# One compact token list less: expert blocks read their token numbers from the regions

## The chip, the cores and the metric

The kernel runs on one core of one Trainium2 chip. The metric is device time in microseconds (us). The kernel before has a median of 954.01 us over 3 runs (950.93 to 955.18).

## The reference

Three stages in a row, for 4 sequences of 576 tokens (2304 tokens, width 512):

```python
# 1: causal attention (8 heads of 64) mixed with a linear memory
out = g * mem_out + (1 - g) * local
# 2: mixture of 8 experts, one expert per token
logits = x @ w_gate + modality_bias[modality_id]
e_idx = np.argmax(logits, axis=1)
for e in range(E):                       # E = 8
    mask = e_idx == e
    h = np.maximum(x[mask] @ w1[e], 0.0)  # 512 -> 1024
    out[mask] = gate_w[mask, None] * (h @ w2[e])
# 3: one dense network for all tokens, 512 -> 2048 -> 512
h = x @ w_in
g = np.where(h > 0.0, h, alpha * (np.exp(np.minimum(h, 0.0)) - 1.0))
return (g @ w_out)
```

Which tokens an expert gets is known only while the kernel runs, so the kernel has to build lists of token numbers and gather rows by them.

## The kernel before

The program is one long stream in three stages: attention (up to about 250 us of the trace), the experts (to about 535 us), the last network (to the end). Matrix products in 32 bits are made of three matmuls on a high and a low part of each operand, which is why there are many "split" steps: ScalarE (ACT) copies the high part, VectorE (DVE) or GpSimd (POOL) subtracts to get the low part.

**Lists.** While attention runs, the router gives each token an expert and a place. All the rows x (512 values and the gate weight) are stored in DRAM as `xd`. The number of each token is scattered into a list in DRAM, `idreg`: every expert has a region of 2560 places (`REG`) in it, and its tokens stand at the front of its region; the rest is zero. That is 18 scatters, one for each 128 tokens, each an indirect DMA from POOL that writes 128 numbers of 4 bytes (`scatter`, L84 to L92). After the first block of the first expert a second list is made in the same way, with 18 more scatters: `idc`, the compact list, in which the experts' tokens follow each other without holes, in the order in which the experts are worked on.

**Blocks.** An expert's tokens are worked on in blocks of 256 columns. For a block the queue of SyncE (SP) loads 256 token numbers into `gi`, POOL issues two indirect gathers of 128 rows each from `xd` into a buffer `xb` (or `xbh`, for the first block of the second expert), ACT and DVE scale the rows by the gate weight (`scale`, L901 and L902), TensorE (PE) turns them (`turn`, L911), and then the first layer (`hidden`, L928 to L931, tiles h and hs, eight steps f) and the second layer (L947, tile acc) run. The result goes to `y` at the block's place in the compact order.

**What else is hung into the blocks.** The functions of a block take lists of other work to be issued after a step. In the first expert's second block (`first(1)`) these are, among others: turning the raw 64-bit words of the last network's weights into 32-bit floats on DVE (`early_bits`, L1236 to L1240, tile T, three instructions for each quarter), and the loads of the second expert's weights (`wload`, L875). The quarter that matters below is loaded by `early_load(3)` (`load_half`, L1228, raw<-in_wout_dram, 512 KB) and used by `early_bits(3)`, which stands in DVE's order between the fifth hidden step's split and the sixth's (L931).

**Order.** All is in the order in which the program is written, per engine; a semaphore wait at the head of an engine's queue holds everything behind it. A DMA that SP issues waits on SP. DMAs from SP and from POOL run on the same 16 DMA engines.

**The last network.** 3 groups of 768 tokens times 16 chunks f of the hidden layer. During the first group each chunk loads the raw weights of the chunk two further on (`load`, fraw, two transfers of 512 KB) into one of two buffers, and DVE turns them (`conv`, L1236 to L1240). At the end of a group the rows are scattered to the output by token number (`finish`, L89, out_dram). The numbers for this, `idi`, are loaded once from `idc` (L1260), before the network's first load.

Of the kernel before, what the change touches and what calls it, by code (L numbers as in the profile page):

```python
# [10 lines left out]
F32 = mybir.dt.float32  # L11
F32R = mybir.dt.float32r
BF16 = mybir.dt.bfloat16
I32 = mybir.dt.int32
AF = mybir.ActivationFunctionType
ALU = mybir.AluOpType
# [68 lines left out]
def scatter(tc, key, dst, idx, src, spare):  # L85

    nc = tc.nc
    nc.gpsimd.memset(spare, 0.0)
    ins = nc.gpsimd.indirect_dma_start(dst, bass.IndirectOffsetOnAxis(ap=idx, axis=0), src, None)  # L89
    ins = ins.ins  # L90
    tc.declare_no_dep(ins, group=key, reason="the rows of the scatters are distinct")
    tc.add_to_no_dep_group(key, ins)  # L92
# [11 lines left out]
def attention_memory_moe_ffn_kernel(  # L104
# [21 lines left out]

    xd = dr.tile([NTOK, ROW], F32, name="xd")
    idreg = dr.tile([E * REG, 1], I32, name="idreg")
    idc = dr.tile([YW, 1], I32, name="idc")

    G = SimpleNamespace(**{k: v for k, v in locals().items() if k != "ctx"})
    ct = lambda name, shape, dt=F32: con.tile(shape, dt, name=name)
# [19 lines left out]
    G.keyE = ct("keyE", [128, E])  # L152
    G.tid = ct("tid", [128, NT], I32)
    G.rpi = ct("rpi", [128, NT], I32)
    G.cpi = ct("cpi", [128, NT], I32)
    G.run = ct("run", [128, E])
    G.spare = ct("spare", [1, 1])
    G.revE = ct("revE", [128, E])
# [4 lines left out]
    def late_constants():  # L163

        nc.gpsimd.memset(G.tri, 0.0)
        nc.gpsimd.affine_select(out=G.tri, in_=G.tri, pattern=[[1, 128]], compare_op=ALU.is_gt, fill=-1.0, base=0, channel_multiplier=-1)
        nc.vector.memset(G.ones, 1.0)
        nc.vector.memset(G.go, 1.0)

        for t0, K in GROUPS:  # L170
            nc.vector.memset(G.go[:, t0 * E : (t0 + K) * E].rearrange("p (e c) -> p e c", e=E)[:, :, 0], 0.0)
        for e in range(E):
            nc.gpsimd.memset(G.revE[:, e : e + 1], float(E - e))
            nc.gpsimd.memset(G.regE[:, e : e + 1], float(e * REG))
            nc.gpsimd.memset(G.iotE[:, e : e + 1], float(e))
            nc.gpsimd.memset(G.keyE[:, e : e + 1], float(e * REG * E + e))
            nc.gpsimd.memset(G.run[:, e : e + 1], float(e * REG))
        for t in range(NT):
            P2, r = divmod(t, 9)
            if r < 8:  # L180
                b, c = 2 * P2 + r // 4, r % 4
                nc.gpsimd.iota(G.tid[:, t : t + 1], pattern=[[0, 1]], base=b * S + 128 * c, channel_multiplier=1)
            else:
                for j in range(2):
                    nc.gpsimd.iota(G.tid[64 * j : 64 * j + 64, t : t + 1], pattern=[[0, 1]], base=(2 * P2 + j) * S + 512, channel_multiplier=1)
        zid = G.tmp[:, 0 : E * REG // 128].bitcast(I32)
        nc.vector.memset(zid, 0)
        nc.sync.dma_start(idreg.rearrange("(p f) o -> p (f o)", p=128), zid)
        nc.sync.dma_start(idc.rearrange("(p f) o -> p (f o)", p=128), zid[:, 0 : YW // 128])

    G.late_constants = late_constants

# [668 lines left out]
def define_experts(tc, G):  # L861
# [22 lines left out]
    def gather_rows(xb, gi, src, rows=NTOK, eng=nc.sync):  # L884
        eng.dma_start(gi, src)
        for h in range(2):
            nc.gpsimd.indirect_dma_start(xb[:, h, :], None, xd[0:rows, :], bass.IndirectOffsetOnAxis(ap=gi[:, h : h + 1], axis=0))  # L887
# [6 lines left out]


    def gather1(xb, gi, start):
        gather_rows(xb, gi, idc[bass.ds(start, BLK), :].rearrange("(p h) o -> p (h o)", h=2))


    def scale(xb):  # L900
# [98 lines left out]

def experts(tc, G, mp):  # L1000
    nc, ct = tc.nc, G.ct
    oh, rk, run, iotE, cpi = G.oh, G.rk, G.run, G.iotE, G.cpi
    wload, wsplit, gather0, gather1, scale, turn, block = G.wload, G.wsplit, G.gather0, G.gather1, G.scale, G.turn, G.block
    t8 = lambda n: ct(n, [128, E])
    key, rank, base, a88, b88 = t8("key"), t8("rank"), t8("base"), ct("a88", [128, E, E]), ct("b88", [128, E, E])
    inner = lambda v: v.unsqueeze(1).to_broadcast([128, E, E])
    outer = lambda v: v.unsqueeze(2).to_broadcast([128, E, E])
    info, infi = ct("info", [128, 3, E]), ct("infi", [128, 3, E], I32)
    nxt, nxti, end, iotJ = ct("nxt", [128, E, 8]), ct("nxti", [128, E, 8], I32), t8("end"), ct("iotJ", [128, 8])
    w, cpf = mp.tile([128, NT, E], F32, name="cw"), ct("cpf", [128, NT])  # L1010
    G.HT.append(mp.tile([128, 4, 2, BLK], F32R, name="hs4"))
    G.HS += [(G.HT[1][:, f, 0], G.HT[1][:, f, 1]) for f in range(4)]
    G.XH, G.XL = [mp.tile([128, 4, BLK], F32R, name=n) for n in ("xh", "xl")]
# [7 lines left out]
    def table_a():  # L1021
        nc.vector.tensor_tensor(run, run, G.regE, op=ALU.subtract)
        nc.vector.scalar_tensor_tensor(key, run, float(E), iotE, op0=ALU.mult, op1=ALU.subtract)
        nc.vector.scalar_tensor_tensor(key, G.first, 65536.0, key, op0=ALU.mult, op1=ALU.add)
        nc.vector.tensor_tensor(a88, inner(key), outer(key), op=ALU.is_gt)
        nc.vector.tensor_reduce(rank, a88, axis=AX.X, op=ALU.add)
        nc.vector.tensor_tensor(a88, a88, inner(run), op=ALU.mult)
        nc.vector.tensor_reduce(base, a88, axis=AX.X, op=ALU.add)
        nc.vector.tensor_tensor(b88, inner(rank), outer(iotE), op=ALU.is_equal)
        for r, src in enumerate((iotE, run, base)):  # L1030
            nc.vector.tensor_tensor(a88, b88, inner(src), op=ALU.mult)
            nc.vector.tensor_reduce(info[:, r], a88, axis=AX.X, op=ALU.add)
        nc.vector.tensor_copy(infi, info)


    def table_b():
        nc.vector.tensor_tensor(key, base, G.regE, op=ALU.subtract)
        for t0, K in GROUPS:
            nc.vector.tensor_tensor(w[:, t0 : t0 + K], oh[:, t0 * E : (t0 + K) * E].rearrange("p (e c) -> p c e", e=E), key.unsqueeze(1).to_broadcast([128, K, E]), op=ALU.mult)
        nc.vector.tensor_reduce(cpf, w, axis=AX.X, op=ALU.add)  # L1040
        nc.vector.tensor_tensor(cpf, cpf, rk, op=ALU.add)
        nc.vector.tensor_copy(cpi, cpf)

        for j in range(8):
            nc.gpsimd.memset(iotJ[:, j : j + 1], float(BLK * (j + 1)))
        nc.vector.tensor_tensor(end, info[:, 1], info[:, 2], op=ALU.add)
        nc.vector.tensor_tensor(nxt, iotJ.unsqueeze(1).to_broadcast([128, E, 8]), info[:, 2].unsqueeze(2).to_broadcast([128, E, 8]), op=ALU.add)
        nc.vector.tensor_scalar(nxt[:, 0], nxt[:, 0], float(FIRST + BLK), None, op0=ALU.add)
        nc.vector.tensor_tensor(nxt, nxt, end.unsqueeze(2).to_broadcast([128, E, 8]), op=ALU.min)
        nc.vector.tensor_copy(nxti, nxt)  # L1050

    why = dict(skip_runtime_bounds_check_because="a count of tokens")
# [5 lines left out]
        G.cnt[u] = nc.values_load(infi[0:1, 1, u : u + 1], min_val=0, max_val=NTOK, **why)  # L1058

    def start_of(u, j):  # L1060
        return nc.values_load(nxti[0:1, u, j : j + 1], engines=[mybir.EngineType.SP], min_val=0, max_val=NTOK, **why)

    P = lambda f, *a: (lambda: f(*a))
    mid1 = {}
# [21 lines left out]
    W[2][0] = G.kp.tile([128, 4096], F32R, tag="k1", name="W20")  # L1086
    load_eid(1)
    gather0(2)
    for t in range(NT):
        scatter(tc, "idc", G.idc, cpi[:, t : t + 1], G.tid[:, t : t + 1], G.spare)  # L1090
    wload(1, 0, 0)
    early_load(2)
    for g in mid2.get(4, ()):
# [1 line left out]
    early_bits(1)  # L1095
    wload(1, 0, 1)
    early_load(3)
    gather1(G.XBH, G.gis[2], nc.values_load(infi[0:1, 2, 1:2], engines=[mybir.EngineType.SP], min_val=0, max_val=NTOK, **why))

    def first(j):  # L1100
        mid1, mid2 = {}, {1: []}
# [141 lines left out]
def ffn(tc, G, ps, fp):  # L1243
# [13 lines left out]
    YL, EE = YL + ring("yk", 1, [4, 384], F32R), EE + ring("ef", 1, [384])  # L1257
    EG = ring("eg", 2, [384])
    GH, GL = ring("gh", 4, [384], F32R), ring("gl", 4, [384], F32R)
    nc.sync.dma_start(idi, idc[0:NTOK, :].rearrange("(t p) o -> p (t o)", p=128))  # L1260

    WS, YS, HP, GG, ACC = {}, {}, {}, {}, {}
    cnt = {}
# [55 lines left out]
    def gsplit(g, f, h):  # L1319
        gg = GG[g, f, h]  # L1320
        gh, gl = rot(GH, "gh"), rot(GL, "gl")
        nc.scalar.copy(gh, gg)
        eng = nc.vector if g and f < 2 or g == NG - 1 and f == NF - 1 else nc.gpsimd
        eng.tensor_tensor(gl, gg, gh.bitcast(F32), op=ALU.subtract)  # L1324
        GG[g, f, h] = (gh, gl)
# [28 lines left out]
    for i, (g, f) in enumerate(seq):  # L1354
        g1, f1 = seq[i + 1] if i + 1 < len(seq) else (NG, 0)
        f2 = f + 2 if g == 0 and f + 2 < NF else None
        if i > WM and g1 < NG:
            wsplit(g1, f1, 0)
        if f2 and f2 > 3:
            load(f2)  # L1360
        mm1(g, f, 0)
        if f2 and i > 1:
            conv(f2, 0)
        elu(g, f, 0)
        if i < 2:
            conv(2, 2 * i)
        if i > 0:
            gsplit(*seq[i - 1], 1)
        if 0 < i <= WM:
            wsplit(g1, f1, 0)  # L1370
        if f2 and i > 1:
            conv(f2, 1)
        mm1(g, f, 1)
        if f == NF - 1 and g + 1 < NG:
            ysplit(g + 1, 1)
        elu(g, f, 1)
        if i < 2:
            conv(2 + i, 1 - i)
        gsplit(g, f, 0)
        if f2 and i > 1:  # L1380
            conv(f2, 2)
        wsplit(g, f, 1, nc.gpsimd if i < WPL else nc.vector)
        if i == 1:
            conv(3, 1)
            conv(3, 2)
        if g + 1 < NG and 10 <= f < 14:
            ysplit(g + 1, 0, (f - 10,))
        if i > 0:
            gp, fp = seq[i - 1]
            if i == len(seq) - 2:  # L1390
                break
            mm2(gp, fp)
            if fp == NF - 1:
                finish(gp)
# [79 lines left out]
```

## Time and profile before

| | |
|---|---|
| median of the runs | 954.01 us (950.93 to 955.18) |
| the profiled execution's own time | 953.88 us |
| its span, first to last instruction | 952.1 us |
| TensorE busy | 878.4 us (92%) |
| VectorE busy | 549.1 us (58%) |
| ScalarE busy | 485.5 us (51%) |
| GpSimd busy | 282.3 us (30%) |
| mean DMA rate | 68 GB/s |
| mean granted TensorE clock | 0.958 of full speed |

TensorE is busy nearly all the time, so what matters is the few places where it stands still, and who ended each of them. The shares of the other engines say little by themselves: each of them waits for TensorE most of the time.

### The profile page before, as it was taken

Reading aid. Unit: us, or ns where it says so; the run is one execution under the profiler, and the core shown is the slowest. Engines: PE = TensorE matmul, PEld = TensorE weight load, DVE = VectorE, ACT = ScalarE, POOL = GpSimd, SP = SyncE. Lnnn points to the kernel's source line nnn. Section 1 sums busy time; section 2 is a strip of 40 time slices with the busy share of each in tenths; the row PEclk is TensorE's granted clock in tenths of the full one; section 3 lists DMA queues with packets and bytes.
Section 4 is the critical chain, followed back from the end, with each engine's and each line's share of the span. In section 5 each row is a group of like instructions: output and inputs, shape, how many; then the busy total and the mean of one; then the engine's idle time right before and its main releaser. Section 6 shows DMA issues by size and latency. Waiting matters only on the chain. (4 is left out here: it accounts for less than half of the span.)

```text
span 952.1 us, 16341 instructions
## 1 busy us (share of the span) xinstructions
PE 878.4 (92%) x6038; PEld 790.8 (83%) x6038; DVE 549.1 (58%) x1270; ACT 485.5 (51%) x1141; POOL 282.3 (30%) x415
## 2 busy tenths in 40 slices
PE   6999999989596999799996799999999999999995
PEld 4888887867495999799984679999999999999995
DVE  7888888976682322352212599787644455544442
ACT  5577776756131222332213565566766566656653
POOL 6443334644445200001000043222422222322223
PEclk8899999999697999799997899999999999999998
DMA  7122423536243600241011233430100000100001
GB/s 190 48 87 87 131 86 100 68 79 187 83 135 44 200 24 24 59 146 47 23 26 27 92 120 129 146 114 23 66 1 1 1 1 1 67 1 1 1 1 66
DMA packets 29553, 65.14 MB, mean 68 GB/s; under 512 B 11008, under 2 KB 11136, under 8 KB 29440
## 3 DMA queue, kind: packets, MB, share of 16 engines
q1 hardware_dynamic: 23520, 49.50, 17.9%
q0 software_dynamic: 4832, 12.14, 4.0%
q10 hardware_dynamic: 1088, 2.10, 0.7%
q8 instruction: 58, 0.95, 0.5%
q14 instruction: 55, 0.45, 0.2%
HBM read 54.14 MB, written 9.58 MB: 67 GB/s over the span
## 5 line engine op out<-in xcount | busy, mean ns | idle before, releaser
L1324 POOL TENSOR_TENSOR gl<-eg,gh 128x384 fp32r<-128x384 f32 x86 | 94.1, 1095 | 273.5 <-PE fh L1305 185.6
L947 PE MATMUL acc<-hs,W 128*128 128x256 f32 x864 | 109.3, 287 | 10.0 <-DVE hs L931 9.9
L947 PEld LDWEIGHTS acc<-hs,W 128*128 128x128 f32 x864 | 106.4, 193 | 10.7 <-DVE hs L931 10.3
L1335 PE MATMUL facc<-wl,gh 128*128 128x512 f32 x288 | 112.6, 391 | 1.0 <-POOL wl L1285 1.0
L1335 PE MATMUL facc<-wh,gl 128*128 128x512 f32 x288 | 112.6, 391 | 0.0
L1335 PE MATMUL facc<-wh,gh 128*128 128x512 f32 x288 | 112.3, 390 | 0.0
L1312 ACT ACTIVATE er<-fh 128x384 f32<-128x384 f32 x96 | 47.1, 491 | 112.5 <-PE fh L1305 109.4
L1305 PE MATMUL fh<-yh,first_w 128*128 128x384 f32 x384 | 99.8, 341 | 4.8 <-ACT yh L1296 4.8
L928 PE MATMUL h<-xh,W 128*128 128x256 f32 x512 | 93.7, 285 | 7.2 <-issue 6.9
L1315 DVE SCALAR_TENSOR_TENSOR ee<-ee,er 128x384 f32<-128x384 f32 x48 | 27.9, 581 | 119.6 <-ACT er L1314 119.6
L450 ACT ACTIVATE sr<-sr,mx 128x512 f32<-128x512 f32 (+3 forms) x128 | 71.7, 562 | 33.2 <-DVE mx L399 31.0
L928 PEld LDWEIGHTS h<-xh,W 128*128 128x128 f32 x512 | 80.5, 193 | 7.6 <-issue 7.1
L887 POOL DMA_INDIRECT xb<-xd,gi x26 | 25.8, 991 | 193.7 <-ACT xh L912 80.6
L930 ACT ACTIVATE hs<-h 128x256 fp32r<-128x256 f32 x72 | 27.5, 384 | 101.2 <-PE h L928 95.6
L1305 PEld LDWEIGHTS fh<-yh,first_w 128*128 128x128 f32 x384 | 71.2, 191 | 7.0 <-ACT yh L1296 5.0
L380 POOL TENSOR_TENSOR heads<-lqk,heads 128x704 fp32r<-128x704 f32 (+1 forms) x31 | 46.2, 1489 | 101.6 <-ACT heads L377 85.8
L928 PE MATMUL h<-xl,W 128*128 128x256 f32 x256 | 73.1, 285 | 0.2 <-DVE xl L913 0.2
L399 DVE CUSTOM_DVE_ANT_0 sr<-s,mb 128x512 f32<-128x512 f32 (+2 forms) x144 | 69.6, 502 | 5.0 <-PE s L431 1.9
L1305 PE MATMUL fh<-yh,wh 128*128 128x384 f32 x192 | 64.5, 336 | 0.9 <-DVE eg L1316 0.9
L484 DVE COPY aT<-t 128x512 f32<-128x512 f32 (+3 forms) x106 | 49.8, 480 | 25.9 <-PE t L472 25.7
L1305 PE MATMUL fh<-yh,wl 128*128 128x384 f32 x192 | 64.4, 336 | 0.1
L931 DVE SCALAR_TENSOR_TENSOR hs<-h,hs 128x256 fp32r<-128x256 f32 x72 | 30.1, 422 | 59.1 <-ACT hs L930 59.1
(339 smaller groups left out, 1996.7 us busy)
## 6 DMA issues: line engine op xcount, KB each, us to landing
raw<-in_w_dram SPq DMA_DIRECT2D x20, 512.0 KB, 4.6
lqk<-in_qk_dram SPq DMA_DIRECT2D x15, 672.0 KB, 4.0
fraw<-in_win_dram SPq DMA_DIRECT2D x14, 512.0 KB, 3.8
fraw<-in_wout_dram SPq DMA_DIRECT2D x14, 512.0 KB, 4.7
vt<-in_vP_dram SPq DMA_DIRECT2D x16, 320.0 KB, 3.0
xd<-early_rows SPq DMA_DIRECT2D x2, 1032.0 KB, 4.6
xd<-late_rows SPq DMA_DIRECT2D x2, 1032.0 KB, 4.9
raw<-in_w_dram ACTq DMA_DIRECT2D x4, 512.0 KB, 6.1
```

What stands on the lines that cost most here:

```text
L380: eng.tensor_tensor(heads[:, p % 2, 1, PART[n]], LD[p % 2][:, PART[n]], heads[:, p % 2, 0, PART[n]].bitcast(F32), op=ALU.subtract)
L399: nc.vector.tensor_tensor_reduce(out=dst, in0=src, in1=mask, scale=-0.125, scalar=start, op0=ALU.add, op1=ALU.min, accum_out=least)
L450: nc.scalar.activation(sr[:, o : o + W], sr[:, o : o + W], AF.Exp, scale=-1.0, bias=mx[:, r : r + 1], accum_out=SUM[p][:, i, j : j + 1])
L484: nc.vector.tensor_copy(dst, src)
L928: nc.tensor.matmul(hp, wt[:, k, 128 * f : 128 * f + 128], xt[:, k, :], start=(k == 0 and r == 0), stop=(k == 3 and r == 2))
L931: nc.vector.scalar_tensor_tensor(hl, hp, 0.0, hh.bitcast(F32), op0=ALU.max, op1=ALU.subtract)
L947: nc.tensor.matmul(o, wt[:, f, 128 * dc : 128 * dc + 128], ht, start=(f == 0 and r == 0), stop=(f == FF // 128 - 1 and r == 2))
L1305: nc.tensor.matmul(hp, wt[:, k, :], xt[:, k, :], start=(k == 0 and r == 0), stop=(k == 3 and r == 2))
L1312: nc.scalar.activation(r, hp, AF.Relu, scale=-1.0)
L1315: nc.vector.scalar_tensor_tensor(e, e, 1.0, r, op0=ALU.add, op1=ALU.mult)
L1324: eng.tensor_tensor(gl, gg, gh.bitcast(F32), op=ALU.subtract)
L1335: nc.tensor.matmul(ACC[g][a], gt[:, c], wt, start=(f == 0 and r == 0), stop=(f == NF - 1 and r == 2))
```

## The change

The compact list is no longer scattered. Every block gathers by its expert's region of `idreg` (`gather1` reads `idreg`; the table `nxti` of the next block's start, made in `table_b`, now holds places in the regions). The 18 scatters into `idc`, the seven DVE instructions that worked out their places, and the zeroing of `idc` at the start go. The list in compact order is still needed at the end, for the output rows. It is put together during the first eight chunks of the last network: `tokens(i)` copies 2304 numbers from the region of the i-th expert to that expert's place in `idc`, each copy overwriting the tail of the one before, and after the fourteenth chunk `idi` is loaded from it.

```diff
-    idc = dr.tile([YW, 1], I32, name="idc")
+    idc = dr.tile([2 * NTOK, 1], I32, name="idc")
...
     def gather1(xb, gi, start):
-        gather_rows(xb, gi, idc[bass.ds(start, BLK), :].rearrange("(p h) o -> p (h o)", h=2))
+        gather_rows(xb, gi, idreg[bass.ds(start, BLK), :].rearrange("(p h) o -> p (h o)", h=2))
...
+        nc.vector.tensor_scalar(info[:, 3], info[:, 0], float(REG), None, op0=ALU.mult)
         nc.vector.tensor_copy(infi, info)
...
     def table_b():
-        nc.vector.tensor_tensor(key, base, G.regE, op=ALU.subtract)
-        for t0, K in GROUPS:
-            nc.vector.tensor_tensor(w[:, t0 : t0 + K], oh[:, t0 * E : (t0 + K) * E].rearrange("p (e c) -> p c e", e=E), key.unsqueeze(1).to_broadcast([128, K, E]), op=ALU.mult)
-        nc.vector.tensor_reduce(cpf, w, axis=AX.X, op=ALU.add)
-        nc.vector.tensor_tensor(cpf, cpf, rk, op=ALU.add)
-        nc.vector.tensor_copy(cpi, cpf)
...
     gather0(2)
-    for t in range(NT):
-        scatter(tc, "idc", G.idc, cpi[:, t : t + 1], G.tid[:, t : t + 1], G.spare)
     wload(1, 0, 0)
...
-    gather1(G.XBH, G.gis[2], nc.values_load(infi[0:1, 2, 1:2], engines=[mybir.EngineType.SP], min_val=0, max_val=NTOK, **why))
+    gather1(G.XBH, G.gis[2], nc.values_load(infi[0:1, 3, 1:2], engines=[mybir.EngineType.SP], min_val=0, max_val=E * REG - BLK, skip_runtime_bounds_check_because="a place in the regions"))
...
-    nc.sync.dma_start(idi, idc[0:NTOK, :].rearrange("(t p) o -> p (t o)", p=128))
+    def tokens(i):
+        if i < E:
+            sp = [mybir.EngineType.SP]
+            a = nc.values_load(G.infi[0:1, 3, i : i + 1], engines=sp, min_val=0, max_val=(E - 1) * REG, skip_runtime_bounds_check_because="a region")
+            b = nc.values_load(G.infi[0:1, 2, i : i + 1], engines=sp, min_val=0, max_val=NTOK, skip_runtime_bounds_check_because="a count of tokens")
+            nc.sync.dma_start(idc[bass.ds(b, NTOK), :].rearrange("n o -> o n"), G.idreg[bass.ds(a, NTOK), :].rearrange("n o -> o n"))
+        if i == NF - 3:
+            nc.sync.dma_start(idi, idc[0:NTOK, :].rearrange("(t p) o -> p (t o)", p=128))
...
         gsplit(g, f, 0)
+        if g == 0:
+            tokens(i)
```

POOL's rows between the first block of the first expert and its second, before (xb, xbh and gi are the gathered rows and their numbers; the 36 rows of MEMSET and scatter repeat):

```order
L887 DMA xb_3416<-xd,gi_107 128x516 x2
L1058 TENSOR_LOAD infi x5
L887 DMA xb_3209<-xd,gi_106 128x516 x2
L88 MEMSET spare 1x1
L89 DMA idc<-tid,cpi 2560x1
...
L1058 TENSOR_LOAD infi x3
L887 DMA xbh<-xd,gi_108 128x516 x2
L1150 COMPARE_AND_BRANCH
L1115 COMPARE_AND_BRANCH
L887 DMA xb_3416<-xd,gi_107 128x516 x2
```

The same place of POOL after the change:

```order
L885 DMA xb_3412<-xd,gi_106 128x516 x2
L1055 TENSOR_LOAD infi x5
L885 DMA xb_3207<-xd,gi_105 128x516 x2
L1055 TENSOR_LOAD infi x3
L885 DMA xbh<-xd,gi_107 128x516 x2
L1145 COMPARE_AND_BRANCH
L1110 COMPARE_AND_BRANCH
L885 DMA xb_3412<-xd,gi_106 128x516 x2
```

The gathers into xbh and into the next xb follow the earlier gathers directly.

SP's rows in the last network after the change, from the first copy on (waits in brackets: DMAHW and DVE name the semaphores that the row waits for):

```order
L1260 TENSOR_LOAD infi
L1261 TENSOR_LOAD infi
L1262 ISA
L1262 DMA idc<-idreg 16x144 [waits DMAHW1_49,DMAHW0_49]
L1221 DMA fraw_14477<-in_win_dram 128x1024 [waits DMAHW4_49,DVE_49]
L1223 DMA fraw_14477<-in_wout_dram 128x1024 [waits DMAHW5_49]
L1260 TENSOR_LOAD infi
L1261 TENSOR_LOAD infi
L1262 ISA
L1262 DMA idc<-idreg 16x144 [waits DMAHW1_49]
L1221 DMA fraw_14478<-in_win_dram 128x1024 [waits DMAHW6_49,DVE_49]
```

These are the second and the third copy; each stands between two chunks' weight loads, is cut into 16 pieces of 576 bytes, and waits for the copy before it.

## Rows read from the trace of the kernel before

**Rows 1.** Who TensorE waited for, 255 to 520 us: total, times, longest

```profile
PE acc L947 <- DVE hs L931: 9.9, 2, 9.4
PE h L928 <- issue: 6.9, 1, 6.9
```

**Rows 2.** TensorE in order of time: start, us, instruction, in brackets idle and releaser

```profile
291.15 2.18 PE L947 MATMUL acc<-hs,W 128*128 128x256 f32 x17
302.78 6.26 PE L947 MATMUL acc<-hs,W 128*128 128x256 f32 x31 [9.45 <-DVE hs L931]
309.66 5.95 PE L947 MATMUL acc<-hs,W 128*128 128x256 f32 x48
```

**Rows 3.** VectorE in order of time, the same stretch

```profile
300.12 0.43 DVE L1236 TENSOR_SCALAR T<-raw 128x512 int32<-128x512 int32 x1 [12.15 <-DMA raw<-in_wout_dram]
...
302.31 1.08 DVE L931 SCALAR_TENSOR_TENSOR hs<-h,hs 128x256 fp32r<-128x256 f32 x3
```

**Rows 4.** SyncE's queue in order of time, the same stretch

```profile
283.34 2.92 SPq L1228 DMA_DIRECT2D raw<-in_wout_dram  x1
313.89 1.41 SPq L885 DMA_DIRECT2D gi<-idc  x2
```

**Rows 5.** DMAs issued from 282 to 290 us: count, KB each, median us to landing

```profile
raw<-in_w_dram SPq DMA_DIRECT2D x1, 512.0 KB, 10.9
raw<-in_wout_dram SPq DMA_DIRECT2D x1, 512.0 KB, 16.8
```

**Rows 6.** DMA issues of the whole span, from the page

```profile
lqk<-in_qk_dram SPq DMA_DIRECT2D x15, 672.0 KB, 4.0
...
idc<-tid,cpi POOLq DMA_INDIRECT x18, 10.2
...
gi<-idc SPq DMA_DIRECT2D x11, 1.0 KB, 2.0
...
idi<-idc SPq DMA_DIRECT2D x1, 9.0 KB, 3.3
```

**Rows 7.** DMAs issued from 182 to 183 us, in attention

```profile
lqk<-in_qk_dram SPq DMA_DIRECT2D x1, 672.0 KB, 13.0
idreg<-tid,rpi POOLq DMA_INDIRECT x1, 17.6
```

**Rows 8.** Busy time by stretch: length, engines' busy us (count), clock, DMA share, GB/s

```profile
278.00:282.00 4.00, 3.53 (x28) 3.10 (x27) 3.15 (x5) 1.46 (x3) 3.51 (x7) 1.00 0.97 362
282.00:286.00 4.00, 4.00 (x36) 4.00 (x35) 2.87 (x7) 1.07 (x3) 3.34 (x7) 1.00 0.40 14
303.00:309.00 6.00, 6.00 (x33) 6.00 (x34) 1.52 (x3) 0.00 (x0) 4.10 (x7) 0.58 0.02 0
309.00:315.00 6.00, 6.00 (x54) 6.00 (x53) 3.02 (x4) 1.08 (x2) 0.00 (x0) 1.00 0.00 0
```

**Rows 9.** TensorE and VectorE one block later

```profile
329.88 3.95 PE L947 MATMUL acc<-hs,W 128*128 128x256 f32 x31 [0.42 <-DVE hs L931]
...
329.01 0.49 DVE L902 TENSOR_SCALAR xb<-xb 128x512 f32<-128x512 f32 x1 [3.61 <-DMA xb<-xd,gi]
```

**Rows 10.** DMAs issued from 539 to 541 us, as the last network starts

```profile
fraw<-in_wout_dram SPq DMA_DIRECT2D x2, 512.0 KB, 7.1
```

**Rows 11.** ScalarE at the border of the first expert, 386 to 392 us

```profile
389.32 0.62 ACT L1160 CAST first_w<-T 128x512 fp32r<-128x512 f32 x1 [6.51 <-PEq L1118]
```

**Rows 12.** SyncE, VectorE and GpSimd in the last network, order of time

```profile
553.50 0.43 SPq L1228 DMA_DIRECT2D fraw<-in_wout_dram  x1
...
560.21 1.52 DVE L1236 TENSOR_SCALAR T<-fraw 128x1024 int32<-128x1024 int32 x1
...
680.21 1.01 POOL L89 DMA_INDIRECT out_dram<-fraw,idi  x1 [2.25 <-ACT fraw L1343]
```

**Rows 13.** DMAs issued from 552 to 555 us

```profile
fraw<-in_wout_dram SPq DMA_DIRECT2D x1, 512.0 KB, 4.5
```

**Rows 14.** SyncE's register loads at L1061: duration ns min, median, max

```profile
L1061 SPq TENSOR_LOAD <-nxti x10: 265/270/275, 314.5 to 469.7; - x10
```

More of the change, by code (lines that the diff above doesn't have):

```diff
@@ L154, in attention_memory_moe_ffn_kernel @@
     G.rpi = ct("rpi", [128, NT], I32)
-    G.cpi = ct("cpi", [128, NT], I32)
     G.run = ct("run", [128, E])
@@ L188, in late_constants @@
         nc.sync.dma_start(idreg.rearrange("(p f) o -> p (f o)", p=128), zid)
-        nc.sync.dma_start(idc.rearrange("(p f) o -> p (f o)", p=128), zid[:, 0 : YW // 128])
     G.late_constants = late_constants
@@ L1001, in experts @@
     nc, ct = tc.nc, G.ct
-    oh, rk, run, iotE, cpi = G.oh, G.rk, G.run, G.iotE, G.cpi
+    run, iotE = G.run, G.iotE
     wload, wsplit, gather0, gather1, scale, turn, block = G.wload, G.wsplit, G.gather0, G.gather1, G.scale, G.turn, G.block
@@ L1007, in experts @@
     outer = lambda v: v.unsqueeze(2).to_broadcast([128, E, E])
-    info, infi = ct("info", [128, 3, E]), ct("infi", [128, 3, E], I32)
-    nxt, nxti, end, iotJ = ct("nxt", [128, E, 8]), ct("nxti", [128, E, 8], I32), t8("end"), ct("iotJ", [128, 8])
-    w, cpf = mp.tile([128, NT, E], F32, name="cw"), ct("cpf", [128, NT])
+    info, infi = ct("info", [128, 4, E]), ct("infi", [128, 4, E], I32)
+    G.infi = infi
+    nxt, nxti, off, iotJ = ct("nxt", [128, E, 8]), ct("nxti", [128, E, 8], I32), ct("off", [128, E, 8]), ct("iotJ", [128, 8])
     G.HT.append(mp.tile([128, 4, 2, BLK], F32R, name="hs4"))
@@ L1032, in table_a @@
             nc.vector.tensor_reduce(info[:, r], a88, axis=AX.X, op=ALU.add)
+        nc.vector.tensor_scalar(info[:, 3], info[:, 0], float(REG), None, op0=ALU.mult)
         nc.vector.tensor_copy(infi, info)
     def table_b():
-        nc.vector.tensor_tensor(key, base, G.regE, op=ALU.subtract)
-        for t0, K in GROUPS:
-            nc.vector.tensor_tensor(w[:, t0 : t0 + K], oh[:, t0 * E : (t0 + K) * E].rearrange("p (e c) -> p c e", e=E), key.unsqueeze(1).to_broadcast([128, K, E]), op=ALU.mult)
-        nc.vector.tensor_reduce(cpf, w, axis=AX.X, op=ALU.add)
-        nc.vector.tensor_tensor(cpf, cpf, rk, op=ALU.add)
-        nc.vector.tensor_copy(cpi, cpf)
         for j in range(8):
             nc.gpsimd.memset(iotJ[:, j : j + 1], float(BLK * (j + 1)))
[L1046 to L1049, printed above, removed]
+        flat = lambda v: v.unsqueeze(2).to_broadcast([128, E, 8])
+        nc.vector.tensor_copy(off, iotJ.unsqueeze(1).to_broadcast([128, E, 8]))
+        nc.vector.tensor_scalar(off[:, 0], off[:, 0], float(FIRST + BLK), None, op0=ALU.add)
+        nc.vector.tensor_tensor(nxt, off, flat(info[:, 3]), op=ALU.add)
+        nc.vector.tensor_tensor(nxt[:, 0 : E - 1], nxt[:, 0 : E - 1], info[:, 3, 1:E].unsqueeze(2).to_broadcast([128, E - 1, 8]), op=ALU.subtract)
+        nc.vector.tensor_tensor(off, flat(info[:, 1]), off, op=ALU.is_gt)
+        nc.vector.tensor_tensor(nxt, nxt, off, op=ALU.mult)
+        nc.vector.tensor_tensor(nxt[:, 0 : E - 1], nxt[:, 0 : E - 1], info[:, 3, 1:E].unsqueeze(2).to_broadcast([128, E - 1, 8]), op=ALU.add)
         nc.vector.tensor_copy(nxti, nxt)
@@ L1060, in start_of @@
     def start_of(u, j):
-        return nc.values_load(nxti[0:1, u, j : j + 1], engines=[mybir.EngineType.SP], min_val=0, max_val=NTOK, **why)
+        return nc.values_load(nxti[0:1, u, j : j + 1], engines=[mybir.EngineType.SP], min_val=0, max_val=E * REG - BLK, skip_runtime_bounds_check_because="a place in the regions")
     P = lambda f, *a: (lambda: f(*a))
```

## The prediction

> **What bounds the kernel now.** I read the table of busy shares first, then the list of waits of TensorE for the experts' stage, then the timelines of the engines around the longest wait. TensorE is busy 92% of the span, so a change to lists, which are the work of POOL, DVE and SP, can only pay where TensorE stands still. In the experts' stage there are few such places [rows 1]: waits of kind "issue" at borders of blocks, and two waits of the second layer for a DVE split, 9.9 us together, 9.4 of them in one piece.
>
> That piece is at 293.33 us. TensorE issues 17 second-layer matmuls, stops for 9.45 us, and goes on at 302.78 [rows 2]. Each hidden step feeds three matmuls, so the 17th is the second one of the sixth step, and the next needs that step's low part. DVE makes that low part in the row at 302.31 [rows 3], and it is late because DVE stood for 12.15 us in front of the quarter T of the last network's weights, until 300.12, for a DMA (raw<-in_wout_dram). SP issued this DMA at 283.34 [rows 4], and it took 16.8 us to land [rows 5]. So the chain is: load late, DVE held, split late, TensorE still.
>
> Why is a load of 512 KB that late? Not for bytes: from 278 to 282 us the DMA engines moved 362 GB/s, from 282 to 286, with this load and its neighbour issued, 14 GB/s [rows 8]. What runs there is the series of 18 scatters of `idc`, 128 numbers of 4 bytes each, with a median of 10.2 us to land [rows 6]. The same pattern is there a second time: when the first scatters of `idreg` run in attention, a load of lqk lands after 13.0 us [rows 7], where the 15 loads of its kind have a median of 4.0 [rows 6]. Two loads of different data, each beside 4-byte scatters, come 9 to 12 us late. I take it that the scatters hold them up.
>
> **What the change removes.** The 18 scatters of `idc` and the POOL rows around them.
>
> (a) *The gap.* Without scatters the load should land as two loads issued back to back do. The nearest row is the start of the last network, where four such loads are issued close together and the two of this kind land after a median of 7.1 [rows 10]: 283.34 + 7.1 = 290.4. The other end is the single load of this kind beside a neighbour in the last network, 4.5 us [rows 13]: 287.8. What TensorE can bear: in the trace 2.66 us pass from the landing (300.12) to its restart (302.78), for three T instructions, a scaling and the split. To cause no gap the load has to land by 293.33 − 2.66 = 290.67. Both ends make it, the upper one by 0.3 us only (the later one of its two loads would not; that belongs to the first rival). The load has one neighbour here, so it is nearer to the lower end, and I take the whole gap as gone: −9.45 us.
>
> (b) *The slow clock behind it.* After the gap the 31 matmuls take 6.26 us, then 48 take 5.95 [rows 2], which is 0.124 each; 31 at that rate are 3.84. The stretch 303 to 309 has a granted clock of 0.58 and the next 1.00 [rows 8], so the first ran mostly at 1.2 and the second at 2.4 GHz. As a check, 33 matmuls against 54 in 6 us make 21 × 0.111 = 2.3. Without the idle time before it I expect no slow clock here: −2.42 us. Bounds: 0, if the clock falls anyway, and −2.42.
>
> (c) *The next block's small wait.* At 329.88 TensorE waits 0.42 us for a split, behind a scaling that waited 3.61 us for the gathered rows [rows 9]. These rows are gathered late because SP stood in front of the gi loads until 313.89 [rows 4], waiting for the scatters. After the change POOL goes from one gather to the next without them, and SP's gi load waits for nothing that is late, so the rows are there up to 27 us earlier (313.89 against the end of its last issue, 286.3): −0.42 us.
>
> **What it adds in the experts' stage.** DVE's table has 1929 rows instead of 1932, small instructions of about 0.2 us beside running matmuls: 0. The gathers read other places of a list that has been complete since attention: 0. But the gathers into xbh and the following xb, four of 128 rows, now run at about 287 us, beside the late load. This is the one place where the change could take back (a); it is the first rival.
>
> A rule of the Trainium skill bears on that: "DMA: Bandwidth & Descriptors", section "Issuing engines are not separate DMA queues", says that transfers issued by POOL and by SP interleave on the same 16 engines, so that gathers moved forward compete with the load. The bytes are two loads and four gathers, about 2.1 MB; at the 362 GB/s of [rows 8] that is an estimate of 5.8 us, landing at 289.1, inside the limit.
>
> **What it adds in the last network.** Eight copies of 9 KB in DRAM on SP's queue, one per chunk, each with two register loads of 0.27 us [rows 14], and a wait for the copy before. Queued behind such a copy is the next chunk's load of fraw; DVE waits for that, and TensorE for DVE. No row shows a copy in DRAM. Nearest from below: a gi load of 1 KB, 2.0 us; the idi load of 9 KB in 4-byte pieces, 3.3; from above, the scatters into DRAM, 10.2 [rows 6]. I take 3.3, since the size is the same. The copy was issued a whole chunk before its successor. From the third chunk's load (553.50) to the first output scatter (680.21, [rows 12]) lie some 15 chunks, 8.4 us each, so at 3.3 us SP does not wait at all. The margin of a load: issued at 553.50, landed 4.5 later at 558.0, used by DVE at 560.21 [rows 12, 13], so 2.2 us. At 10.2 per copy SP would fall behind by 1.8 us per chunk, 12.6 us by the eighth copy; it is idle for the rest of a chunk, so a load comes too late only beyond 8.4 + 2.2 = 10.6, by 2 us at the end. I cost the copies at 0, with 2 us at the upper end. The idi load, now behind the fourteenth chunk, is needed at 680.21 by the first output scatter, three chunks or 25 us later: 0.
>
> **Does the gain last?** What comes after hangs on TensorE. At the border of the first expert ACT waits for PE's branch (6.51 us, [rows 11]) and TensorE's 6.9 us of "issue" [rows 1] follow that, so the border moves with the matmuls. The last network is held by TensorE and DVE, and its loads by DVE. I see no fixed point downstream.
>
> **Sum.** −9.45 − 2.42 − 0.42 = −12.29 us. The profiled execution's own time is 953.88 us (span 952.1), 0.13 below the median of the runs; 953.88 − 12.29 = 941.6, and on the median 941.7 us.
>
> **Rivals.**
>
> *The load still comes late, in part.* The gathers of four times 128 rows and the second expert's loads, which SP now issues that much earlier, meet the load at 283 to 291 us. For it: the small margin at the upper row. Against it: rows with 362 GB/s. If it took the 10.9 us of the neighbour issued just before it [rows 5], it would land at 294.2, 3.6 us late; with up to 2.4 of slow clock the time would be 945.3 to 947.7.
>
> *The scatters are not the cause.* Then load and gap stay and only (c) is won: 953.6. For it: scatters carry 512 bytes each, and the load's own issue took 2.92 us on SP [rows 4], so something in the queue itself was slow. Against it: lqk beside scatters [rows 7]. [...]
>
> *Slower: the copies disturb the loads of the last network.* Six copies stand beside a load (the third to the eighth). If a copy of small pieces delayed its load as the scatters did, from 4.5 to 16.8 us, each of six chunks would lose 12.3 − 2.2 = 10.1 us, 61 us in all, against a gain of 12.3: 1002 us. It is slower than before from 12.3 / 6 = 2.0 us per chunk, that is, from a load that takes 4.5 + 2.2 + 2.0 = 8.7 us. Against it: a copy has 16 pieces of 576 bytes, the series of scatters 2304 pieces of 4.
>
> **How the numbers follow.** The forecast 0.76, its own range 937.5 to 944: below, the runs of before reach 3.1 us under their median (950.93), and code at the borders may fetch a little differently. Late load 0.12, up to 947.7. Scatters not the cause 0.07, 953.6. Slower 0.05. The range 937.5 to 948 takes in the first two, 0.88 in all, less what the unknown sizes leave out. A measurement of this kernel tells about 0.5% from no change: faster means under 949.2, slower over 958.8. So faster 0.88, same 0.07, slower 0.05.
>
> **What would show it.** Step by step in the profile after: no row of `idc` scatters between 278 and 307 us; raw<-in_wout_dram issued at about 283 and landing within 4.5 to 7.1 us; no wait of TensorE for the split of the second layer above 0.5 us; a granted clock of 1.00 from 290 to 315; the gathers into xbh at about 287 to 291 instead of 318.80; the end of that block near 303 instead of 315; and fraw loads in the last network still landing in about 4.5 us, with no DVE wait for them. The prediction is wrong in its cause if the load takes over 8 us without the scatters beside it, and wrong in its sum if the block ends 12 us earlier and the whole does not.

## The result, and the profile after

The changed kernel takes 939.82 us (median of 4 runs, 937.47 to 942.1), the kernel before 954.6 us in the same comparison (4 runs, 950.93 to 956.09). The ratio is 0.9851, its 95% interval 0.9813 to 0.9888. The forecast was 941.7 us, range 937.5 to 948. The profiled execution took 942.1 us, its span 940.3 us.

First the waits of TensorE from 245 to 505 us, the whole list (us in total, times, longest).

```profile
engine line waited for: us in total, times, longest us
PE r_ps L675 <- DVE oh L664: 10.1, 1, 10.1
PE h L926 <- issue: 6.7, 1, 6.7
PE q L962 <- issue: 2.3, 1, 2.3
PE t L909 <- DVE xb L900: 1.1, 1, 1.1
PE qt L969 <- ACT xb L965: 0.3, 1, 0.3
PE h L926 <- ACT xh L910: 0.2, 1, 0.2
PE h L926 <- DVE xl L911: 0.2, 1, 0.2
```

The line with acc (now L945) and hs, 9.9 us in [rows 1], is gone; the other large waits are there as before (that for r_ps is 10.1 us in the trace of before too, ahead of the window of [rows 1]). The timeline of TensorE around the place (start, duration, operation, count):

```profile
293.49 5.76 PE L945 MATMUL acc<-hs,W 128*128 128x256 f32 x48
299.09 1.03 PE L909 MATMUL t<-ident,xb 128*128 128x128 f32 x8
299.88 5.86 PE L945 MATMUL acc<-hs,W 128*128 128x256 f32 x48
```

All 48 matmuls of the first half now run as one piece of 5.76 us, where before there were 17, a stop of 9.45 us, and 31 more [rows 2]. The load that had come late, on SP's queue, and then DVE's use of it:

```profile
285.14 0.33 SPq L873 DMA_DIRECT2D raw<-in_w_dram  x1
285.57 0.38 SPq L1223 DMA_DIRECT2D raw<-in_wout_dram  x1
```

```profile
290.26 0.42 DVE L1231 TENSOR_SCALAR T<-raw 128x512 int32<-128x512 int32 x1
290.71 0.69 DVE L1233 SCALAR_TENSOR_TENSOR T<-raw,T 128x512 int32<-128x512 int32 x1
```

It was issued at 285.57 and DVE started on it 4.7 us later without a wait, so it landed within 4.7 us, against 16.8 in [rows 5]; the issue itself takes 0.38 us where it took 2.92 [rows 4].

The stretches of [rows 8] (PE, PEld, DVE, ACT and POOL busy with counts, granted clock, DMA share, GB/s):

```profile
282.00:286.00 4.00, 3.78 (x32) 3.68 (x32) 3.33 (x7) 0.80 (x3) 0.00 (x0) 1.00 0.49 181
303.00:309.00 6.00, 6.00 (x55) 6.00 (x54) 1.16 (x3) 0.77 (x2) 1.78 (x2) 1.00 0.24 69
309.00:315.00 6.00, 6.00 (x56) 6.00 (x55) 3.82 (x6) 3.92 (x7) 0.12 (x1) 1.00 0.46 152
```

The clock is 1.00 where it was 0.58. The gather into xbh, at 318.80 us before, now runs here, and waits only for its own list:

```profile
290.97 1.25 POOL L885 DMA_INDIRECT xbh<-xd,gi  x1 [9.72 <-DMA gi<-idreg]
```

The copies in the last network (duration in ns min/median/max, first and last start; then their time to landing, all of tile idc):

```profile
L1262 SPq DMA_DIRECT2D idc<-idreg x8: 531/536/714, 528.2 to 581.8; - x8
L1264 SPq DMA_DIRECT2D idi<-idc x1: 1480/1480/1480, 629.1 to 629.1; - x1
...
DMA to landing us min/median/max: 3.2/3.2/7.3
```

Nothing waits for them, and DVE's list of waits there holds no DMA.

The whole is easier to judge by stages. **A** runs from the start of the span to ScalarE's branch into the first expert's second block, **B** is the second and the third block, **C** goes from there to the first matmul of the last network, **D** to the last output scatter. All of the profiled executions, in us, worked out from the starts of these instructions in each trace; a kernel's number is that of its group in the next section:

```
                              A      B      C      D
before           (1st)      280.0   54.8  203.7  404.9
changed          (1st)      282.5   40.8  202.3  407.5
before again     (3rd)      284.7   54.7  203.3  404.3
changed again    (3rd)      287.8   40.6  203.9  406.6
load early       (2nd)      287.3   55.6  204.5  404.4
scatters kept    (2nd)      287.5   62.8  203.8  407.7
18 reads         (2nd)      285.8   67.2  203.7  407.4
18 rows of 512 B (2nd)      286.5   67.1  203.2  407.7
no copies        (3rd)      289.3   40.6  204.1  406.6
72 memsets       (3rd)      287.9   42.6  203.8  406.0
9 reads          (4th)      281.5   40.9  205.0  406.0
9 reads, spaced  (4th)      276.2   40.8  205.2  405.4
18 plain, by SP  (4th)      280.1   49.7  203.3  406.1
18 reads, block 4 (4th)     281.3   40.9  204.1  406.2
```

Between the first two rows B gives 14.0 us. C gives 1.4, and A and D take back 2.5 and 2.6: 10.3 in all in these two executions. Another 1.5 us lie behind D, where POOL ends with a DRAIN instruction: it takes 8.15 us before and 6.66 after, which makes the 11.8 us by which the two spans differ. This DRAIN goes with the number of indirect transfers that POOL issued in the whole program: 8.15 and 8.14 us with 82 (kernel before, scatters kept), 7.40 with 73 (9 reads), 6.66 and 6.67 with 64 (changed, memsets, plain writes by SP). The medians differ by 14.8.

### The profile page after: what moved, and what is told of

The parts are those of the page before. It is cut to its first block, busy times and chain, and to the rows that moved or that the text cites. A ratio compares the mean times of both kernels' runs of the same rounds, so it can differ in the third digit from the quotient of the medians.

```text
span 940.3 us, 16356 instructions
## 1 busy us (share of the span) xinstructions
PE 879.7 (94%) x6038; PEld 791.0 (84%) x6038; DVE 551.5 (59%) x1267; ACT 485.6 (52%) x1141; POOL 263.8 (28%) x379
## 5 line engine op out<-in xcount | busy, mean ns | idle before, releaser
L945 PE MATMUL acc<-hs,W 128*128 128x256 f32 x864 | 105.3, 281 | 0.0
L945 PEld LDWEIGHTS acc<-hs,W 128*128 128x128 f32 x864 | 103.0, 189 | 0.0
L926 PE MATMUL h<-xh,W 128*128 128x256 f32 x512 | 91.7, 283 | 6.9 <-issue 6.7
L482 DVE COPY aT<-t 128x512 f32<-128x512 f32 (+3 forms) x106 | 49.8, 480 | 25.0 <-PE t L470 24.8
```

What stands on the lines that cost most here:

```text
L482: nc.vector.tensor_copy(dst, src)
L926: nc.tensor.matmul(hp, wt[:, k, 128 * f : 128 * f + 128], xt[:, k, :], start=(k == 0 and r == 0), stop=(k == 3 and r == 2))
L945: nc.tensor.matmul(o, wt[:, f, 128 * dc : 128 * dc + 128], ht, start=(f == 0 and r == 0), stop=(f == FF // 128 - 1 and r == 2))
```

## The experiments

Theory A at first: scatters of 4-byte numbers make a load beside them late, and the late load is the whole gap. Each group ran beside the kernel before; since the kernel before took 954.6, 964.0, 962.5 and 955.5 us in the four comparisons, groups are compared by ratios and by column B.

**Scatters kept.** The changed kernel with 18 scatters back in the old place.

```diff
     gather0(2)
+    for t in range(NT):
+        scatter(tc, "idz", G.idz, G.rpi[:, t : t + 1], G.tid[:, t : t + 1], G.spare)
     wload(1, 0, 0)
```

> The changed kernel with 18 scatters of 4-byte numbers put back on POOL in the old place, into a list that nobody reads; the blocks still gather by the regions and no instruction waits for this list. Theory A (the scatters hold up the load beside them): raw<-in_wout_dram lands 12 to 17 us after its issue again, TensorE stops 8 to 10 us before the second block's second layer at a low clock afterwards, and the time is 950 to 955 us (ratio to before 0.995 to 1.00). Rival B (what cost the time was SP and POOL waiting for the compact list, not the scatters' own traffic): the load lands in about 5 us, no gap, 938 to 943 us.

Measured: 974.48 us, ratio 1.0112 (1.0076 to 1.0149). The scatters by themselves take back all of the gain, and more. The load is late again (issued at 290.60, DVE waits for it until 310.11), but DVE's waits from 286 to 330 us show that it is the smaller part:

```profile
DVE y L949 <- remote: 12.8, 1, 12.8
DVE hs L930 <- ACT hs L929: 9.1, 2, 8.1
DVE hs L930 <- issue: 3.9, 1, 3.9
DVE T L1234 <- DMA raw<-in_wout_dram: 3.2, 1, 3.2
```

"Remote" and "issue" mean that nothing in the trace released the instruction. TensorE's timeline in the same block has the same thing within one row of matmuls that wait for nothing between them:

```profile
319.52 0.64 PE L946 MATMUL acc<-hs,W 128*128 128x256 f32 x4 [1.13 <-issue]
320.94 0.63 PE L946 MATMUL acc<-hs,W 128*128 128x256 f32 x4 [0.78 <-issue]
322.37 0.81 PE L946 MATMUL acc<-hs,W 128*128 128x256 f32 x3 [0.80 <-issue]
```

**Load early.** The kernel before, with the late load issued ahead of the scatters (at 284.48 us; the first scatter follows at 285.97).

```diff
     early_load(2)
+    early_load(3)
...
     wload(1, 0, 1)
-    early_load(3)
```

> The kernel before, with one line moved: the load raw<-in_wout_dram for the fourth quarter is issued right behind its neighbour raw<-in_win_dram (about 277 us, before the scatters of idc start at 278.8) instead of at 283. All scatters and the compact list stay. Theory A: this load lands by about 284, DVE no longer stands before it, and the gap of 9.45 us with its 2.4 us of low clock goes: 941 to 945 us (ratio 0.985 to 0.991). Rival C (some other thing late behind it, such as the second expert's weights or the gathers behind the scatters, takes its place): a new TensorE wait of several us in the same block or the next, 946 to 954 us.

Measured: 962.14 us, ratio 0.9984 (0.996 to 1.0008). DVE no longer waits for the load, and nothing is gained. The second block is 6 to 7 us shorter (24.1 us from branch to branch, 30.0 and 31.0 in the two traces of the kernel before), and the third 7 to 8 longer (31.5 against 24.8 and 23.7). SP's queue, then ScalarE and DVE say why:

```profile
284.48 0.37 SPq L1228 DMA_DIRECT2D raw<-in_wout_dram  x1
290.03 0.34 SPq L875 DMA_DIRECT2D raw<-in_w_dram  x1
322.80 1.42 SPq L885 DMA_DIRECT2D gi<-idc  x2
324.47 2.17 SPq L875 DMA_DIRECT2D raw<-in_w_dram  x4
```

```profile
328.39 1.04 ACT L881 CAST W<-raw 128x1024 fp32r<-128x1024 f32 x1 [5.69 <-DMA raw<-in_w_dram]
329.47 1.23 DVE L882 TENSOR_TENSOR W<-raw,W 128x1024 fp32r<-128x1024 f32 x1 [6.31 <-issue]
```

The gather's list gi cannot be loaded until the scatters of idc have landed (322.80), and the second expert's weights stand behind it in SP's order. They are issued at 324.47, ScalarE waits for them until 328.39, the split of W follows at 329.47, and TensorE waits 4.6 us for the hs behind it, the longest wait of that block. The second block is not free either: ScalarE stands there for 7.30 us ("remote") and TensorE for 3.73 ("issue"), and its 24.1 us compare with 17.8 in the changed kernel. So the scatters reach the blocks by at least two ways, and taking one away uncovers the next. One thing limits this run: it belongs to the second group, where engines stop without a releaser; in the trace that the prediction read they did not. What the moved load alone would give in such an execution was not run, though SP's gi loads waited for the scatters there as well, until 313.89 [rows 4].

**18 reads** and **18 rows of 512 bytes**: the changed kernel with another kind of transfer in the old place.

```diff
+        nc.gpsimd.indirect_dma_start(G.probe[:, t : t + 1], None, G.idreg[:, :], bass.IndirectOffsetOnAxis(ap=G.rpi[:, t : t + 1], axis=0))
...
+        scatter(tc, "idz", G.idz, G.rpi[:, t : t + 1], G.ident, G.spare)
```

> The changed kernel with 18 indirect gathers of 128 numbers of 4 bytes (read from the regions' list in DRAM into a small tile that nobody uses) in the place where the scatters were. Same count of POOL instructions, indices and pieces as the scatters, but 4-byte reads instead of 4-byte writes in DRAM. Theory A1 (small writes in DRAM are what is slow): the load lands in 5 to 7 us, no gap, 938 to 943 us. Rival A2 (any 2304 small pieces that POOL puts into the queues hold up SP's loads): the load lands after 10 us or more and a gap of 4 to 10 us returns, 945 to 955 us.

> The changed kernel with 18 scatters in the old place that write rows of 512 bytes (128 rows each, 1.2 MB in all) instead of 4-byte numbers, into a DRAM tensor that nobody reads. Theory A1 in its narrow form (pieces under 512 bytes are the trouble): the load is delayed only by the bytes, 1.2 MB at 200 to 360 GB/s is 3 to 6 us spread over 28 us, so it lands in 5 to 8 us and the time is 938 to 943 us. Rival A3 (scatters from POOL hold up the loads whatever their size): the load lands after 12 us or more, 950 to 955 us.

Measured: 975.45 us (1.0113, 1.0068 to 1.0158) and 975.74 us (1.0124, 1.0083 to 1.0166). In both, the load is on time as far as the traces tell: neither gives this load's time to landing, and DVE takes it up only at 319.56 and 320.26 us, without a wait. But SP's queue (q1: packets, MB, share of 16 engines) moves the 1.05 MB of the load and its neighbour, issued from 288.44 and 289.20 us on, within 7 and 6 us; with reads from 288 to 295 us, with long rows from 289 to 295:

```profile
q1 hardware_dynamic: 576, 1.05, 47.3%
q1 hardware_dynamic: 576, 1.05, 51.6%
```

And yet B is 67 us. So the half of theory A on the load stood (reads and long rows do not delay it), and the other half fell: a punctual load did not give the gain. Both times lie above every range that was given, the rivals' too. What stands there instead, in the kernel with reads, is ScalarE first, then DVE and TensorE, while POOL issues from 284.85 to 312.26 us:

```profile
293.07 0.38 ACT L929 ACTIVATE hs<-h 128x256 fp32r<-128x256 f32 x1 [7.76 <-remote]
312.03 0.38 ACT L929 ACTIVATE hs<-h 128x256 fp32r<-128x256 f32 x1 [18.57 <-issue]
312.45 0.42 DVE L930 SCALAR_TENSOR_TENSOR hs<-h,hs 128x256 fp32r<-128x256 f32 x1 [18.53 <-issue]
```

```profile
293.97 0.79 PE L927 MATMUL h<-xh,W 128*128 128x256 f32 x2 [4.09 <-issue]
...
297.95 0.57 PE L927 MATMUL h<-xl,W 128*128 128x256 f32 x1 [0.34 <-issue]
312.93 0.79 PE L927 MATMUL h<-xh,W 128*128 128x256 f32 x2 [14.41 <-DVE hs L930]
```

```profile
295.00:305.00 10.00, 2.41 (x9) 1.75 (x8) 0.00 (x0) 0.00 (x0) 8.24 (x16) 0.50 0.02 0
```

TensorE had issued the block's matmuls from 284.88 to 289.60 us with hardly a stop, some three hidden steps at the 1.41 us that one takes in the changed kernel; ScalarE took up the first at 293.07 and the second at 312.03. In ten of these microseconds DVE and ScalarE do nothing at all, and the DMA engines are busy 2%: it is not bandwidth. Why B grows by 22 to 27 us in these three runs, where the scatters of the kernel before cost 14, is not answered.

**Before again, changed again, no copies, 72 memsets.**

```diff
-        if i < E:
+        if i < 0:
...
-        if i == NF - 3:
+        if i < 0:
...
-            scatter(tc, "out", out, idi[:, t : t + 1], ob, G.spare)
+            scatter(tc, "out", out, G.tid[:, t : t + 1], ob, G.spare)
```

```diff
     gather0(2)
+    for t in range(NT):
+        for r in range(4):
+            nc.gpsimd.memset(G.probe, float(t))
```

> The kernel before, unchanged, for its trace beside the others. Theory S (the 18 scatters themselves hold up the other engines, by the load in one run and by late instructions or signals in another): about 954 to 966 us, with a stretch of 7 to 12 us in which TensorE stands between the branch into the second block and its end, whatever ends it. Theory C (the stalls seen in the kernels with added transfers come from their own added code): the gap is again the one of [rows 1], 9 to 10 us behind the load of raw, and nothing else stands.

> The changed kernel, unchanged, beside the others. Both theories: 0.985 of the kernel before (0.981 to 0.989 where it was measured first), so 940 to 950 us, no wait of TensorE on hs in the second block, that block 23.5 to 24.5 us long.

> The changed kernel without the eight copies in DRAM and without the load of idi, the numbers of the last scatter taken from tid (so the rows of the output are not in the reference's order). Theory N (the copies lie beside work and cost nothing): the same time as the changed kernel within 1.5 us. Rival K (SP's two register loads and the copy in front of each of the first loads of a network cost the last network time; the changed kernel gave back 1 to 1.5 us there): 1 to 3 us below the changed kernel, all of it behind 525 us.

> The changed kernel with 72 memsets of 256 numbers a partition on POOL in the place of the 18 scatters (POOL busy some 15 to 25 us, no transfer). Theory P (a POOL that is busy in that place is what holds the others, because the gathers and branches behind it come late): 10 to 35 us over the changed kernel, with the same stops of ScalarE, VectorE and TensorE in the second block as beside the 18 reads. Theory D (it takes transfers that POOL issues): within 2 us of the changed kernel as long as the gathers of the next block still land before their use, and no stop in the second block.

Measured against 962.51 us for the kernel before: changed 947.78 (0.9833, 0.9775 to 0.9891), no copies 945.49 (0.9825, 0.9782 to 0.9868), memsets 948.67 (0.9849, 0.9798 to 0.9899). The kernel before took 957.41 in the one run that was traced.

The trace of the unchanged kernel before is the surprise. DVE does not wait for the late load, and TensorE and ScalarE stand all the same, in the pattern of the reads; its waits of TensorE from 250 to 345 us:

```profile
PE h L928 <- DVE hs L931: 6.3, 1, 6.3
PE h L928 <- issue: 3.9, 6, 1.7
```

The load was late there too, as its issue and DVE's first use of it show:

```profile
287.77 1.64 SPq L1228 DMA_DIRECT2D raw<-in_wout_dram  x1
304.02 0.42 DVE L1236 TENSOR_SCALAR T<-raw 128x512 int32<-128x512 int32 x1
```

The last signal of its landing in the records of this trace stands at 303.94 us, 16.2 us after the issue; the stop had only kept DVE from coming sooner. B is 54.7 us there and 54.8 in the trace that the prediction read. The price of the scatters was the same in both, and its form was not. Theory S held.

The memsets keep POOL busy for 27.23 us in the same place, and only the gathers behind them come late, at 315.34 us, which costs B 2 us: a busy POOL is not what stops the others. It takes transfers.

Without the copies D is 406.6 us in the one trace, as in the one with them; that speaks against rival K, which puts the cost there. The medians do not decide: they differ by 2.3 us, as K has it, but the two sets of runs overlap (943.63 to 949.37 without, 940.67 to 948.52 with).

**How many, how dense, from whom, and where.** The changed kernel with 9 of the reads; with the 9 spaced by four memsets each; with 18 plain writes on SP's queue; with the 18 reads inside the fourth block.

```diff
+    for t in range(NT // 2):
+        nc.gpsimd.indirect_dma_start(G.probe[:, t : t + 1], None, G.idreg[:, :], ...)
+        for r in range(4):                      # spaced alone
+            nc.gpsimd.memset(G.pad, float(t))
...
+    for t in range(NT):                         # by SP, behind the load of gi
+        nc.sync.dma_start(G.idz[128 * t : 128 * t + 128, :], G.tid[:, t : t + 1])
...
+        if j == 3:
+            mid1.setdefault(1, []).append(reads)
```

> The changed kernel with 9 of the 18 indirect 4-byte reads that POOL issues, back to back, in the place of the old scatters. Theory R (while POOL issues indirect transfers back to back the other engines stand, so the price goes with the length of the series): 11 us of series, 8 to 17 us over the changed kernel, half of what the 18 reads cost (975.5 against 947.8, some 28 us). Rival T (it takes a series longer than some ten, at which the queue is full): under 3 us over the changed kernel.

> The same 9 reads, each followed by four memsets on POOL (some 1.6 us), so that the series takes some 26 us instead of 11. Theory R (back to back is what does it): under 4 us over the changed kernel. Rival Q (each such transfer has its price, however they are spaced): the same 8 to 17 us as the 9 reads in a row. Rival T: under 3 us, as the 9 in a row.

> The changed kernel with 18 plain 4-byte writes of tid into an unread list, issued by SP behind the load of the next gather's list (so behind the loads of raw), none by POOL. Theory R (transfers that POOL issues): within 3 us of the changed kernel. Rival W (small packets on the transfer engines hold up whatever else goes through them, whoever issues them): 10 to 35 us over it, with stops of ScalarE, VectorE and TensorE in the second block.

> The changed kernel with the 18 indirect reads in a row not in front of the second block but inside the fourth (behind its gather, some 330 us into the span), where no load of raw or weights runs beside them. Theory R (the series holds the engines wherever it stands): 20 to 35 us over the changed kernel, with the stops in the fourth block. Rival L (the place matters: it needs the branch into a new block and the loads beside it): under 6 us over the changed kernel.

Measured against 955.45 us: 9 reads 942.16 (0.9866, 0.9838 to 0.9894), spaced 943.07 (0.9884, 0.9862 to 0.9905), 18 plain writes 947.3 (0.9919, 0.9889 to 0.9949), 18 reads in the fourth block 940.63 (0.9834, 0.9792 to 0.9875).

Nine reads stop nothing, back to back or spaced, and 18 in the fourth block stop nothing either, which theory R had put at 20 to 35 us (and the nine at 8 to 17). That block, with POOL as busy as in the row of the 18 reads above:

```profile
325.00:335.00 10.00, 10.00 (x90) 10.00 (x90) 2.42 (x6) 1.99 (x6) 8.23 (x16) 1.00 0.15 42
335.00:345.00 10.00, 10.00 (x89) 10.00 (x88) 2.75 (x6) 2.00 (x5) 8.26 (x16) 1.00 0.02 0
```

So a series of transfers by POOL is not enough. What else it needs is open: the place (loads beside it, a block just entered), the number, and the group of runs all differ between the two 18-read runs. The group may well be part of it. While the 18 scatters of idreg ran in attention, which both kernels have, the engines stood as well in the second and third groups; in the first and fourth they hardly did. The stretch 179 to 195 us of the changed kernel in the third group:

```profile
179.00:195.00 16.00, 10.53 (x75) 7.97 (x72) 8.09 (x27) 6.89 (x22) 12.39 (x19) 0.91 0.67 65
```

and of the kernel with 18 reads in the fourth block:

```profile
179.00:195.00 16.00, 15.56 (x169) 12.81 (x165) 14.45 (x39) 10.20 (x32) 14.25 (x24) 1.00 0.77 68
```

TensorE has 5.0 us more work in the second, and column A is 6.5 us shorter. Most of A's spread goes with the group, and so does most of the 7 to 9 us by which the kernel before differs between these two pairs of groups. The chip does not explain it: the record has the third and the fourth group on a chip of the same number (11), the second on another (8). What differs is not known. Neither 18 reads in the old place in a group like the first and fourth, nor 9 in one like the second and third, was run, so the reads of the fourth group do not decide between R, Q, T and L.

The plain writes by SP test the prediction's own step. The load of raw is issued at 283.2, ahead of them all, and now DVE waits for it until 292.86, 9.7 us from its issue; the next weights, behind the 18 in SP's order, come late too. DVE, 286 to 320 us:

```profile
DVE W L881 <- ACT W L880: 6.2, 1, 6.2
...
DVE T L1234 <- DMA raw<-in_wout_dram: 4.9, 1, 4.9
```

B is 8.8 us longer: 2.5 of them in the second block, where the load is, and 6.3 in the third, where the weights are. TensorE and DVE have no long stop without a releaser. So theory R (within 3 us) and rival W (10 to 35, with stops) both missed: the nine runs take 940.88 to 952.36 us, their median is 4 to 7 above those of the other three of this group. That 4-byte writes can hold up a load beside them is shown, for POOL's scatters and in one trace for SP's plain writes.

## Why the prediction came out right, point by point

**(a) The gap, −9.45 us.** It went, and the load landed within 4.7 us, near the lower end of the 4.5 to 7.1 that were given. That the scatters delay the load is borne out twice: with scatters put back it is late, with 4-byte writes by SP it is late, with reads, memsets or 512-byte rows it is not. But the step that made the load *the* cause of the gap is only half true. In the trace that the prediction read, DVE did wait for it; yet it is one of several delays that the same scatters make. With the load moved and the scatters left, the time did not change (0.9984), and in another execution of the same kernel the stop is as long with no wait for the load. The sum came out because the change removes the scatters themselves, hence every one of these ways.

**(b) The slow clock, −2.42 us.** Right: 1.00 in both stretches. Between the starts of the hidden part of the second and the third block lie 23.98 us (281.59 to 305.57) where there were 36.22 (279.23 to 315.45): −12.24, against −11.87 forecast for (a) and (b).

**(c) The small wait, −0.42 us.** Gone. The order of SP's gi load behind the scatters, which the prediction priced at this 0.42 alone, was worth much more once the gap did not cover it: the "load early" run won 6 to 7 us in the second block and lost them again to that very order.

**The table and the gathers in the experts' stage, 0.** Right: no new wait, with the gathers into xbh at 290.97, the time that was forecast. The rival in which they delay the load fell, and so did the one in which the scatters are not the cause.

**The copies, 0.** Right in the result, as far as one trace of each shows, and in the size: 3.2 us in the median and 7.3 at most, 3.3 taken. The longest fraw load is 8.4 us, where the trace of before has 8.0 as its longest and [rows 13] 4.5 as a typical one; no wait followed, and the run without copies is the same in D. The slower rival fell.

**A term left out.** The sum has nothing for POOL's closing DRAIN, which the 18 scatters less make 1.5 us shorter.

**Does the gain last?** In column C yes. That the sum came this close is partly luck: B alone gave 14.0 us against the 12.29 of the whole sum, the two profiled executions differ by 11.8, the medians by 14.8. The remaining differences were not forecast and partly cancel: the fourth block takes 23.0 us in the traces of the changed kernel and its variants and 23.7 in those of the kernel before, and D is 0.5 to 3.4 us longer in all eleven traces of the first kind than in the three of the second, without the copies too. The change touches neither the fourth block's code nor the last network's matmuls; why the matmuls there run at a slightly different pace in the two programs was not found out.

## What to carry to other kernels

When a wait ends on a late load, ask what else the thing that made it late is holding: moving the load away gained nothing here, while removing the 18 scatters of single numbers gained 1.5%. Before building on a gap in one trace, look at a second execution of the same kernel; it had about the same length in both (9.45 us, and 6.3 + 3.9) and another name. Eight copies of some 9 KB between lists in DRAM brought no wait beside a stage that TensorE holds, where a scatter of the same numbers by POOL in front of a block had cost 14 us.

## What was not expected of the hardware

- A series of 18 indirect transfers by POOL, even of 4-byte reads that nobody waits for, left ScalarE and DVE standing for 18.57 and 18.53 us, with no releaser in the trace and the DMA engines busy 2%, and TensorE behind them for 14.41. The same series in the fourth block of a run of another group left TensorE busy 10.00 of 10.00 us. What makes the difference is open.
- With the series in front of it, a row of matmuls that wait for nothing was issued in pieces of two to four, 1.4 us apart. One packet of the queue that carries instructions, 16 KB, took 8.9 us in the same trace, where the 58 such packets of the changed kernel have a median of 1.1 and at most 3.2. But it ran from 304.7 to 313.6 us, before these pieces, which begin at 317.4, and the kernel with reads stops longer without a slow packet there; that instructions come late is not shown.
- Plain 4-byte writes on SP's queue, 18 times 128, took 19.67 us to issue and let a 512 KB load that was issued before them reach DVE only 9.7 us after its issue, where DVE has it within 4.7 us in the changed kernel.
- POOL's DRAIN at the end of the program takes 8.15 us with 82 indirect transfers issued in the whole program, 7.40 with 73 and 6.66 with 64: 83 ns for each.
